# Attention and feed-forward in one kernel: values loaded two heads at a time, smaller steps, a second accumulator tile and a new list

## The chip, the cores and the metric

One core of a Trainium2 chip runs the whole program. A core has five engines, each with its own queue of instructions that it works off in order: TensorE (PE, matrix products, results in PSUM), VectorE (DVE), ScalarE (ACT), GpSimd (POOL) and SyncE (SP, which here issues every DMA). [...] The metric is the device time of the program in microseconds, median of the runs.

## The reference

Eight batches of windowed attention with eight heads of 64, 576 positions. Heads 0 to 3 see the 32 latest keys, heads 4 to 7 see every fourth of the latest 128. The attention's output goes through a two-layer feed-forward with float64 weights.

```python
scores = scale * np.matmul(q, k.transpose(0, 1, 3, 2))
mask_plain = (rel >= 0) & (rel < window)
mask_dil = (rel >= 0) & (rel < window * dilation) & (rel % dilation == 0)
scores = np.where(masks[None, :, :, :], scores, -1000000000.0)
attn = np.exp(scores - np.max(scores, axis=-1, keepdims=True))
attn = attn / (np.sum(attn, axis=-1, keepdims=True) + 1e-09)
x = np.matmul(attn, v)            # then laid out as [4608, 512]
h = x @ w_in                      # 512 -> 2048
g = h * np.tanh(softplus(h))
return (g @ w_out)                # 2048 -> 512
```

## The kernel before

The work is cut into 16 units, each half a batch: 288 positions, all eight heads. The plain heads are kind 0 (three blocks of 96 queries), the dilated ones kind 1 (four blocks, one for each residue). A unit runs through named steps. `ld` loads queries and keys, `lv` the values, `sp` makes the scores (PE), `sc` takes their maximum off (DVE), `ex` is the exponential (ACT), `tp` turns the probabilities, `va` multiplies them with the values (PE) and divides by their sum, `tx` turns the result into x, `ff` is the first layer (24 matmuls of 288 columns for each of eight steps). Up to unit 2 the second layer is `gt` and `fo` (four times 48 matmuls); from unit 3 on it is `ga`, `gq` and `fq`: seven products of half-size matrices in place of eight, of 144 columns each, on sums of weights (`su`) made once.

Units 0 to 2 are "direct": their probabilities and values are float32 and are turned on PE, since the weights are still being prepared. From unit 3 on both are split in two float16 parts and turned by a DMA transpose. Weights come as float64 and are made into two float16 parts in steps: `wl` loads, `wm` and `ws` find a scale, `ww` shifts words together (DVE L408, L410), `wp` splits (ACT L417, DVE L419). All this happens while the first units run.

What stands where in each engine's queue is set by hand: ORDER is a list of step names, and each name runs its generator to the next `yield`. A number behind `=` names the PSUM tile (of four, `b`) that the step takes. `kw` steps are matmuls of zeros that keep PE at work while it has nothing else.

The lines that the prediction speaks of: L494 and L497 load values; for each unit of half the positions that is 12 or 16 DMAs of 64 floats a row. In direct units L508 then copies them on POOL into rows of 65 with a one behind, so that one matmul also gives the sum. L573 are the scores, L598 and L599 the maximum and its subtraction, L606 and L608 the exponentials, L673 the values' matmuls, L681 to L689 the sum, its reciprocal and the quotient, L725 to L732 x of direct units, L715 to L720 x of the others. L773 is the first layer, L779 its Mish, L861 to L863 the gate of the first three units. L912 are the seven products, with three accumulators side by side in one PSUM tile; L926 (ACT) and L931 (DVE) read them into y. L961 is the second layer of units 0 to 2.

## Time and profile before

| what | us |
|---|---|
| median of 3 runs (lowest, highest) | 910.73 (908.52, 910.88) |
| the profiled execution | 902.42 |
| its span | 900.5 |
| PE busy in it | 848.4 (94%) |
| DVE busy | 638.4 (71%) |
| ACT busy | 472.4 (52%) |

The profiled execution is 8.3 us below the median of the timed runs, and 1.9 us above its own span. Durations below come from it. "Busy" of PE counts its matmuls, warming ones too; a wait is shown beside the instruction that waited, with the engine and line that ended it.

### The profile page before, as it was taken

What the parts mean: (1) busy time and instruction counts of PE and PEld (TensorE: products, weight loads), DVE (VectorE), ACT (ScalarE), POOL (GpSimd) and SP (SyncE); (2) the same over time, 40 slices, a digit from 0 to 9 for tenths busy, and PEclk for the clock granted to TensorE, in tenths of its full rate; (3) what the DMA queues carried; (4) which work ended last, traced back from release to release, by engine and by line L of the source; (5) the groups of instructions that cost most, each with busy time, mean ns of one, the idle gap of its engine ahead of it and who ended that gap; (6) DMA issues with size and microseconds to landing.
All of it is one profiled execution on the core that took longest, in us unless ns stands there. A gap on an engine that the chain in (4) does not pass through costs nothing. (4 is left out here: it accounts for less than half of the span.)

```text
span 900.5 us, 32620 instructions
## 1 busy us (share of the span) xinstructions
PE 848.4 (94%) x14897; PEld 724.8 (80%) x14897; DVE 638.4 (71%) x871; ACT 472.4 (52%) x641; POOL 101.6 (11%) x102
## 2 busy tenths in 40 slices
PE   6779998989999999999999899999999899999998
PEld 4656777867788888888887688888888788888987
DVE  5778977746899995878787858675778475744453
ACT  3364744652476565574745545545465275533342
POOL 6356452100000010000000100000000000000000
PEclk7889999999999999999999989999999899999999
DMA  9894252544321564356153443445252512210001
GB/s 278 245 257 117 92 177 59 105 120 119 71 52 19 124 143 87 92 121 136 41 127 82 116 71 66 108 90 108 59 110 73 93 41 51 52 36 23 15 15 41
DMA packets 194986, 86.33 MB, mean 96 GB/s; under 512 B 170272, under 2 KB 190752, under 8 KB 194848
## 3 DMA queue, kind: packets, MB, share of 16 engines
q1 hardware_dynamic: 194848, 84.25, 39.2%
q8 instruction: 116, 1.90, 0.9%
q14 instruction: 22, 0.18, 0.1%
HBM read 56.89 MB, written 9.44 MB: 74 GB/s over the span
## 5 line engine op out<-in xcount | busy, mean ns | idle before, releaser
L773 PE MATMUL b<-x,w 128*128 128x288 f16 x3072 | 400.2, 287 | 1.9 <-ACT den L683 0.5
L773 PEld LDWEIGHTS <-w 128*128 128x128 f16 x3072 | 294.4, 98 | 78.3 <-issue 3.2
L912 PE MATMUL b<-g,w 128*128 128x144 f16 x2496 | 166.6, 226 | 6.1 <-DVE y L931 4.5
L912 PEld LDWEIGHTS <-w 128*128 128x128 f16 x2496 | 158.4, 98 | 10.0 <-issue 6.3
L779 ACT ACTIVATE hm<-b,fs 128x576 f32<-128x576 f32 x128 | 92.4, 735 | 116.5 <-PE b L773 99.0
L886 DVE SCALAR_TENSOR_TENSOR g<-hm,sg,g 128x1152 f16<-128x1152 f32 (+1 forms) x104 | 130.9, 1270 | 31.5 <-PE b L773 16.5
L884 ACT ACTIVATE g<-hm,sg 128x1152 f16<-128x1152 f32 (+1 forms) x104 | 116.2, 1128 | 45.8 <-PE b L912 30.6
L931 DVE SCALAR_TENSOR_TENSOR y<-b,fo,y 128x144 f32<-128x144 f32 x78 | 33.5, 476 | 73.1 <-PE b L912 48.9
L926 ACT ACTIVATE y<-b,fo 128x288 f32<-128x288 f32 x52 | 40.5, 782 | 81.6 <-PE b L912 68.8
L476 POOL COPY qp<-qn 128x576 f32<-128x576 f32 x15 | 27.9, 1862 | 461.1 <-DMA qn<-in_qT 352.6
L892 DVE TENSOR_TENSOR hm<-hm 128x576 f32<-128x576 f32 x104 | 78.8, 769 | 0.9
L961 PE MATMUL b<-g,w 128*128 128x288 f16 x576 | 73.6, 286 | 2.7 <-ACT den L683 2.7
L961 PEld LDWEIGHTS <-w 128*128 128x128 f16 x576 | 55.6, 98 | 17.1 <-issue 2.9
L912 PE MATMUL b<-g,late_sums 128*128 128x144 f16 x936 | 68.4, 231 | 0.7 <-DVE y L931 0.7
L912 PE MATMUL b<-g,g 128*128 128x144 f16 x936 | 67.2, 227 | 1.3 <-issue 0.8
L912 PEld LDWEIGHTS <-late_sums 128*128 128x128 f16 x936 | 62.9, 100 | 1.9 <-DVE y L931 1.1
L912 PEld LDWEIGHTS <-g 128*128 128x128 f16 x936 | 61.0, 98 | 3.4 <-issue 1.7
L715 ACT CAST x<-xs 96x384 f16<-96x384 f32 (+1 forms) x52 | 29.1, 560 | 47.0 <-DMA x<-x 33.5
L687 DVE RECIPROCAL rec<-den 96x6 f32<-96x6 f32 (+1 forms) x64 | 12.0, 187 | 50.7 <-ACT den L683 46.2
L717 DVE TENSOR_TENSOR x<-xs,x 96x384 f16<-96x384 f32 (+1 forms) x52 | 32.1, 617 | 21.4 <-ACT x L715 21.4
L689 DVE TENSOR_TENSOR xs<-b,rec 96x384 f32<-96x384 f32 (+1 forms) x64 | 39.7, 621 | 6.9 <-PE b L725 1.1
L673 PEld LDWEIGHTS <-pT 64*32 64x32 f16 (+1 forms) x3276 | 30.0, 91 | 16.5 <-issue 8.1
(125 smaller groups left out, 838.9 us busy)
## 6 DMA issues: line engine op xcount, KB each, us to landing
qn<-in_qT SPq DMA_DIRECT2D x15, 576.0 KB, 4.5
vn<-in_vd SPq DMA_DIRECT2D x132, 64.0 KB, 2.8
raw<-in_w_out SPq DMA_DIRECT2D x16, 512.0 KB, 4.9
out_T<-y SPq DMA_DIRECT2D x26, 288.0 KB, 2.4
raw<-in_w_in SPq DMA_DIRECT2D x12, 512.0 KB, 4.9
vn<-in_v SPq DMA_DIRECT2D x28, 144.0 KB, 2.7
knd<-in_kdT SPq DMA_DIRECT2D x14, 224.0 KB, 3.2
vn<-in_v SPq DMA_DIRECT2D x24, 128.0 KB, 2.6
```

The lines of the kernel that those rows point to most:

```text
L673: nc.tensor.matmul(avv[s * SQ:(s + 1) * SQ, h, t], p[:hk.stop - hk.start], vv[vi][hk, window(d, kind, t, s), a, :], start=(i == 0), stop=( ...
L689: nc.vector.tensor_tensor(xs[:, :nb].rearrange("p j (h e) -> p h j e", h=2), avv[:, :, :, :D], rc.unsqueeze(3).broadcast_to([QB, 2, nb, D] ...
L717: nc.vector.tensor_tensor(lo, xs[:, :nb], hi, op=ALU.subtract)
L773: nc.tensor.matmul(ph[:, h, :HT], w1[j][:, c, wi, k * P:(k + 1) * P], x_of(d, xi, c), start=(n == 0), stop=(n == len(seq) - 1))
L779: nc.scalar.activation(d["m"][p][:, half, k0:k0 + 2], ph[:, :, :HT], AF.Mish, scale=d["fs"][:, j:j + 1])
L884: nc.scalar.activation(hi, src, AF.Identity, scale=sg)
L886: nc.vector.scalar_tensor_tensor(lo, src, sg, hi, ALU.mult, ALU.subtract)
L892: nc.vector.tensor_tensor(a, a, b, op=op)
L912: nc.tensor.matmul(acc[e], left(l, e, p, wi)[:, k * P:(k + 1) * P], right(gi, k), start=(n in opens and p == 0 and q == 0), stop=(last and ...
L926: nc.scalar.activation(into(half, t), by(acc), AF.Identity, scale=fo)
L931: nc.vector.scalar_tensor_tensor(o, by(acc)[:, e], fo, o, ALU.mult, ALU.add)
L961: nc.tensor.matmul(po[:, :HT], w2[:, e, j, wi, k * P:(k + 1) * P], d["g"][j][:, gi, k, :], start=(j == 0 and n == 0), stop=(j == NCH - 1 a ...
```

## The change

Values are loaded with one descriptor for two heads (128 floats in a row). A window's row now is one, 64 values, 64 values, one (VW = 130 wide), so both heads have their column of ones at an end, and direct units load straight into it: the copy on POOL is gone. Probabilities are laid out by head, then block. Scores stop after two blocks (a `yield`), values are made by blocks with both heads and both pairs together: three steps `va` in place of four (kind 0 whole, kind 1 in two pieces), each with a `yield` behind every block; x likewise. For units 0 and 1 the maximum is taken off by a matmul into PSUM with an identity, and the exponential reads PSUM. The warming matmuls multiply float32 ones, and there are 59 in place of 220. The seven products stand in another order, and one of the three accumulators has a PSUM tile of its own in every unit (before: in the last unit only). ORDER is new.

```diff
+    VW = 2 * (D + 1)
+    APART = range(16)
+    PE_MAX = (0, 1)
...
         if d["direct"]:
-            vn = w2[:, :2].rearrange("p e j i n -> p (e j i n)").bitcast(F32)[:, :NW * 2 * D]
+            vh = pool.tile([P, NW, VW], F32, tag="vh", name="vf", bufs=2)[:, :sum(nw)]
+            nc.gpsimd.memset(vh[:, :, ::VW - 1], 1.0)
+            vn = vh[:, :, 1:VW - 1]
...
-        for h in range(2):
-            for a in range(2):
-                c = (2 * a + h) * D
-                row = v[b, half * (HT - WIN), c:c + D]
-                o = vn[h * WK:(h + 1) * WK, :, a]
...
-        nc.gpsimd.tensor_copy(vh[:, :, :, :D], vn)
+        for a in range(2):
+            o = vn[a * WK:(a + 1) * WK]
+            row = v[b, half * (HT - WIN), 2 * a * D:2 * (a + 1) * D]
+            nc.sync.dma_start(o[:, :n0], bass.AP(row.tensor, row.offset, [[w, WK], [SQ * w, n0], [1, 2 * D]]))
+            yield
...
+        if u in PE_MAX:
+            yield
+            for h in range(2):
+                nc.tensor.matmul(pt[:QB, h, :n * w].rearrange("p (g k) -> p g k", k=w), ident[:QB, :QB],
+                                 nm[:, h, :n].unsqueeze(2).broadcast_to([QB, n, w]), start=False, stop=True,
+                                 skip_group_check=True)
+            d["src", kind], d["dst", kind] = src, dst
+        else:
+            nc.vector.tensor_tensor(dst, src, nm[:, :, :n].unsqueeze(3).broadcast_to([QB, 2, n, w]), op=ALU.add)
...
+    def span(p):
+        return (1, 2 * p - 2, 2 * p) if p else (0, 0, NPB)
...
-    PRODUCTS = (("11", 0, 0, 0), ("12", 0, 1, 2), (0, 3, 0, 1), (1, 2, 0, 0), (2, 3, 1, 0), (3, 1, 0, 1), ("22", 2, 1, 0))
+    PRODUCTS = (("12", 0, 1, 2), ("11", 0, 0, 0), (0, 3, 0, 1), (1, 2, 0, 0), (3, 1, 0, 1), (2, 3, 1, 0), ("22", 2, 1, 0))
...
-        apart = u == NU - 1
+        apart = u in APART
...
-            po[n:] = [take("b", banks)] * (3 - n) if n or not apart else [take("b", banks)] + po[1:]
+        if p == 0 and n == 0:
+            po[1:] = [take("b", banks)] * 2
+            if not apart:
+                po[0] = po[1]
+        if p == 0 and n == 1 and apart:
+            po[0] = take("b", banks)
...
-            nc.tensor.matmul(spare, zeros, zeros[:, :WIDE_MAX], start=not spared, stop=True, skip_group_check=True)
+            nc.tensor.matmul(spare, ones.broadcast_to([P, P]), ones.broadcast_to([P, WIDE_MAX]), start=not spared, stop=True, skip_group_check=True)
...
 ORDER = """
-wl0.0.1 wm0.0.1 mf ld0 ww0.0.1 qp0 ld0 mf cs1 kw43 sp0.0=0 cs0 wl0.0.0 ld0 ld0 ww0.0.0 ww0.0.1 wm0.0.0 ww0.0.1 ld1
+wl0.3.0 wl0.3.1 ld0 ld0 wm0.3.0 wl0.0.0 wm0.3.0 mf ww0.3.0 ww0.3.0 cs1 cs0 wm0.3.1 ld0 ld0 wl0.0.1 ww0.3.0 ww0.3.0
...
```

The first place is SP's queue at the program's start, which decides when the first values land. Before (`raw` are weights, `qn`/`qk` queries of units 0 and 1, `knp` and `knd` keys, `w_90` the place where values of direct units waited):

```order
L343 DMA raw<-in_w_in 128x512 x2
L461 DMA qn<-in_qT 128x1152
L466 DMA knp<-in_kT 128x2x288
L343 DMA raw<-in_w_in 128x512 x2
L470 DMA knd<-in_kdT 128x4x80 x2
L461 DMA qk<-in_qT 128x1152
L466 DMA knp<-in_kT 128x2x320
L343 DMA raw<-in_w_in 128x512 x2
L470 DMA qk<-in_kdT 128x4x112 x2
L494 DMA w_90<-in_v 64x8x64
L497 DMA w_90<-in_vd 64x4x64 x2
```

And SP's queue of the changed kernel, from its start (`vf` are the values in their final place):

```order
L347 DMA raw<-in_w_in 128x512 x4
L465 DMA qn<-in_qT 128x1152
L470 DMA knp<-in_kT 128x2x288
L347 DMA raw<-in_w_in 128x512 x2
L474 DMA knd<-in_kdT 128x4x80 x2
L347 DMA raw<-in_w_in 128x512 x2
L499 DMA vf<-in_v 64x8x128
L503 DMA vf<-in_vd 64x4x128 x2
L499 DMA vf<-in_v 64x8x128
L503 DMA vf<-in_vd 64x4x128 x2
L465 DMA qk<-in_qT 128x1152
L470 DMA knp<-in_kT 128x2x320
```

Two weight pieces (four DMAs) now stand ahead of the first queries, a fourth piece ahead of the values, and unit 1's queries and keys behind unit 0's values instead of ahead; the values are six DMAs in place of twelve.

The second place is DVE's queue where unit 0's attention ends: reciprocals and quotients of the values, and the lower halves of x, on which the first layer waits. Before:

```order
L687 RECIPROCAL rec<-den 96x2x3
L689 TENSOR_TENSOR xs<-b_73,rec 96x2x3x64
L687 RECIPROCAL rec<-den 96x8
L689 TENSOR_TENSOR xs<-b_72,rec 96x2x4x64
L687 RECIPROCAL rec<-den 96x2x3
L689 TENSOR_TENSOR xs<-b_71,rec 96x2x3x64
L408 SCALAR_TENSOR_TENSOR w_89<-w_89,raw 128x512
L687 RECIPROCAL rec<-den 96x8
L689 TENSOR_TENSOR xs<-b_70,rec 96x2x4x64
L410 SCALAR_TENSOR_TENSOR raw<-raw,w_89 128x1024
L732 TENSOR_TENSOR x<-b_72,x 128x4x3x24
L732 TENSOR_TENSOR x<-b_73,x 128x288
```

Now:

```order
L700 RECIPROCAL rec<-den 96x2x4
L702 TENSOR_TENSOR xs_636<-b_73,rec 96x512
L423 SCALAR_TENSOR_TENSOR w_89<-raw,ws_314,w_89 128x2x512
L414 SCALAR_TENSOR_TENSOR raw<-raw,w_86 128x1024
L598 TENSOR_REDUCE nm<-b_71 96x2x6
L412 SCALAR_TENSOR_TENSOR w_87<-w_87,w_90 128x1024
L700 RECIPROCAL rec<-den 96x2x4
L702 TENSOR_TENSOR xs_684<-b_72,rec 96x512
L412 SCALAR_TENSOR_TENSOR w_87<-w_87,w_90 128x1024
L743 TENSOR_TENSOR x<-b_70,x 128x2x192
L743 TENSOR_TENSOR x<-b_73,x 128x576
L743 TENSOR_TENSOR x<-b_72,x 128x2x192
```

More weight work (L412, L414, L423, which were L408, L410, L419) stands between the quotients, and a reduction of unit 1's scores is followed by no subtraction.

The third place is DVE's queue in unit 14, where the accumulators of the products are read into y. Before, all reads of a unit name one tile:

```order
L892 TENSOR_TENSOR hm<-hm 128x4x144
L886 SCALAR_TENSOR_TENSOR g_98<-hm,sg,g_98 128x1152
L931 SCALAR_TENSOR_TENSOR y<-b_73,fo,y 128x2x72 x2
L886 SCALAR_TENSOR_TENSOR g_100<-hm,sg,g_100 128x1152
L886 SCALAR_TENSOR_TENSOR g_99<-hm,sg,g_99 128x576
L931 SCALAR_TENSOR_TENSOR y<-b_73,fo,y 128x2x72 x2
L892 TENSOR_TENSOR hm<-hm 128x4x144
L886 SCALAR_TENSOR_TENSOR g_99<-hm,sg,g_99 128x576
L886 SCALAR_TENSOR_TENSOR g_97<-hm,sg,g_97 128x1152
L892 TENSOR_TENSOR hm<-hm 128x4x144 x2
L931 SCALAR_TENSOR_TENSOR y<-b_73,fo,y 128x2x72 x2
```

Now they name two:

```order
L949 SCALAR_TENSOR_TENSOR y<-b_71,fo,y 128x2x72 x2
L900 SCALAR_TENSOR_TENSOR g_100<-hm,sg,g_100 128x1152
L900 SCALAR_TENSOR_TENSOR g_99<-hm,sg,g_99 128x1152
L949 SCALAR_TENSOR_TENSOR y<-b_71,fo,y 128x2x72 x2
L900 SCALAR_TENSOR_TENSOR g_98<-hm,sg,g_98 128x576
L906 TENSOR_TENSOR hm<-hm 128x4x144
L900 SCALAR_TENSOR_TENSOR g_100<-hm,sg,g_100 128x1152
L906 TENSOR_TENSOR hm<-hm 128x4x144 x2
L900 SCALAR_TENSOR_TENSOR g_101<-hm,sg,g_101 128x1152
L900 SCALAR_TENSOR_TENSOR g_98<-hm,sg,g_98 128x576
L906 TENSOR_TENSOR hm<-hm 128x4x144
L949 SCALAR_TENSOR_TENSOR y<-b_73,fo,y 128x2x72 x2
```

Of four PSUM tiles a unit's products now hold two, and the reads of one no longer stand against matmuls into the other.

## Rows read from the trace of the kernel before

**Rows 1.** The page: busy time of each engine, its share of the span, instructions.

```profile
PE 848.4 (94%) x14897; PEld 724.8 (80%) x14897; DVE 638.4 (71%) x871; ACT 472.4 (52%) x641; POOL 101.6 (11%) x102
```

**Rows 2.** Busy time by stretch (start:end, length, PE, PEld, DVE, ACT, POOL, clock, DMA share, GB/s).

```profile
0.00:45.40 45.40, 31.19 (x767) 25.30 (x768) 29.82 (x45) 16.93 (x26) 21.61 (x39) 0.81 0.90 261
45.40:120.70 75.30, 67.44 (x991) 51.21 (x989) 64.32 (x97) 45.32 (x65) 38.09 (x19) 0.95 0.56 162
120.70:311.00 190.30, 181.91 (x2883) 147.97 (x2882) 152.41 (x204) 100.58 (x137) 24.46 (x20) 1.00 0.38 90
311.00:870.00 559.00, 541.73 (x9855) 474.56 (x9853) 376.85 (x508) 298.74 (x405) 17.42 (x26) 0.99 0.36 79
```

**Rows 3.** Timeline of PE: start, length, line, tiles, count, the idle time before.

```profile
29.98 1.40 PE L673 MATMUL b<-vf,pp 64*32 64x65 f32 x108 [1.49 <-POOL vf L508]
...
45.37 0.41 PE L773 MATMUL b<-x,w 128*128 128x288 f16 x2
...
120.74 6.04 PE L961 MATMUL b<-g,w 128*128 128x288 f16 x48
```

**Rows 4.** Timeline of POOL: the copy of unit 0's values.

```profile
28.03 1.89 POOL L508 COPY vf<-w 128x2048 f32<-128x2048 f32 x1 [9.79 <-DMA w<-in_vd]
```

**Rows 5.** Timeline of SP: first and last issue of unit 0's twelve value loads.

```profile
14.61 0.64 SPq L494 DMA_DIRECT2D w<-in_v  x1
...
24.38 1.68 SPq L497 DMA_DIRECT2D w<-in_vd  x2
```

**Rows 6.** Busy time around these loads.

```profile
12.00:20.00 8.00, 6.74 (x193) 4.54 (x192) 6.01 (x10) 2.15 (x5) 5.70 (x11) 0.65 1.00 281
20.00:28.00 8.00, 5.61 (x177) 4.80 (x175) 7.09 (x7) 3.99 (x5) 0.00 (x0) 1.00 0.77 124
```

**Rows 7.** Groups by line and shape: busy us, mean ns, idle before.

```profile
L419 DVE SCALAR_TENSOR_TENSOR w<-raw,ws,w 128x1024 f16<-128x1024 f32 x14 | 18.5, 1338 | 1.1 <-ACT w L417 1.0
...
L408 DVE SCALAR_TENSOR_TENSOR w<-w,raw 128x1024 int32<-128x1024 int32 x13 | 16.2, 1258 | 10.9 <-POOL raw L406 10.1 <-POOL w L363 0.7
...
L991 PE MATMUL b<-zeros 128*128 128x96 f16 x220 | 15.4, 243 | 6.4 <-DVE wm L384 3.1 <-ACT den L681 1.4 <-DVE zeros L984 1.0
...
L673 PE MATMUL b<-vf,pp 64*32 64x65 f32 x504 | 8.3, 230 | 5.3 <-POOL vf L508 3.5 <-issue 1.8
...
L599 DVE TENSOR_TENSOR sb<-b,nm 96x1024 f32<-96x1024 f32 x3 | 3.7, 1221 | 0.1
...
L599 DVE TENSOR_TENSOR sb<-b,nm 96x768 f32<-96x768 f32 x3 | 2.9, 954 | 0.2
...
L561 PE MATMUL b<-m_b,ident_b 96*96 96x512 bf16 x6 | 2.2, 455 | 2.3 <-POOL m_b L272 1.3 <-DVE x L732 1.0
```

**Rows 8.** Timeline of ACT: a table load and the instruction behind it.

```profile
98.72 1.28 ACT L779 ACT_TABLE_LOAD   x1
100.02 1.37 ACT L779 ACTIVATE hm<-b,fs 128x576 f32<-128x576 f32 x2
```

**Rows 9.** Who PE waited for: us in total, times, longest.

```profile
PE b L673 <- DMA pT<-p: 5.4, 2, 4.5
PE b L912 <- DVE y L931: 5.2, 8, 1.0
...
PE b L573 <- DMA knd<-in_kdT: 2.8, 1, 2.8
```

**Rows 10.** Busy time behind PE's wait at 711.

```profile
711.00:717.00 6.00, 5.54 (x148) 4.81 (x149) 4.29 (x5) 1.43 (x3) 0.47 (x2) 0.50 0.58 120
717.00:723.00 6.00, 6.00 (x160) 5.08 (x159) 0.98 (x4) 3.04 (x5) 0.00 (x0) 0.97 0.41 93
```

**Rows 11.** Timeline of SP ahead of that wait: value loads, then the keys' load.

```profile
702.96 0.62 SPq L494 DMA_DIRECT2D vn<-in_v  x1
703.64 2.41 SPq L497 DMA_DIRECT2D vn<-in_vd  x3
706.09 0.61 SPq L470 DMA_DIRECT2D knd<-in_kdT  x1
```

## The prediction

> **What bounds the kernel now.** First the page's busy times: PE is busy 94% of the span and no other engine over 71% [rows 1]. So time can only be won where PE waits, runs at the low clock or does filler. The view by stretch shows where that is [rows 2]. Up to the first matmul of the first layer at 45.4 [rows 3] PE is busy 31.2 us at a mean clock of 0.81, and 15.4 us in all are warming matmuls [rows 7]. From there to the first matmul of the second layer at 120.7 it idles 75.3 - 67.4 = 7.9 us, at 0.95, while DVE is busy 64.3 of 75.3 us, 85%. Between 120.7 and 311 it idles 8.4, and between 311 and 870, 17.3 us. The start is bound by the way of data and weights through POOL, ACT and DVE, the rest by PE, with waits strewn in. The list of waits names the ones that count [rows 9]: two on a turned probability tile (5.4 us, one of them 4.5), eight of a product's matmul on DVE reading y (5.2), one on keys (2.8).

> **The start.** The way to the first layer begins with unit 0's values. Before, their twelve loads are issued from 14.61 to 26.06 [rows 5], 0.95 us each, the transfers slow from 281 to 124 GB/s meanwhile [rows 6], the POOL copy starts at 28.03 [rows 4] and the first values' matmul at 29.98 [rows 3]. Now there is no copy and there are six loads. Against that stand two things. Ahead of the values SP has 2.1 MB of the last weight group, so the first scores come later: 3.0 MB up to unit 0's plain keys, of which the old order needed 1.9, and the 281 GB/s of rows 6 make the difference 4 us. And the loads now wait for POOL to write the ones, which stands behind a weight piece in POOL's queue; that I put at 17 us. Six issues at 0.95 end at 22.7, and landing took 2 us in rows 4 and 5 (26.06 to 28.03): 25 us for the last value. But unit 1's queries and keys (1.4 MB, 5 us at 281 GB/s) are loaded behind them, and on PE unit 1's dilated scores stand ahead of the last third of unit 0's plain values. That gives 30 for these scores, 31 for the third, 32.2 for DVE's reduction of the scores.

> From there I count DVE's queue, with the durations of the same forms before (1.34 and 1.26 us for a weight instruction, 0.95 and 1.22 for a score one, and so on) [rows 7]. Up to the last lower half of unit 0's x it has 14 instructions, 10.8 us: x is whole at 43, against 45.4 to 47.5, when the old one's first layer began and its x was done. Little is won there. More is won behind it: up to the second half of the first output weights, without which the second layer cannot go far, the new queue has 85 instructions, 65.8 us, so 55.0 behind x. DVE at the 85% of rows 2 takes 64.4 us for them: 107.5. PE has less to do in that time: 384 matmuls of the first layer at 0.126 us, the pace of the 48 in rows 3, are 48 us, and the scores, values and turns of units 1 and 2 are small beside that. So the second layer begins at 107.5 in place of 120.7. The old list had then also made unit 2's values and x (84 matmuls of two records each at 8.3 / 504 = 0.0165 us [rows 7], 2.8 us, and 14 float32 transposes, which I put at 1.5), which the new one has ahead of it: 120.7 - 4.3 - 107.5 = 8.9 us. I take 8; the bounds are 18, with a DVE that never idles, and 0, with one busy 75%. What shortens the queue is the subtraction of the maximum in units 0 and 1, 2 x (1.22 + 0.95) = 4.3 us of DVE [rows 7], and that weights which waited for values now stand ahead of them.

> What the start pays on PE: eight identity matmuls of 384 or 512 float32 columns. The trace has none. The nearest below is the bfloat16 one of 512 columns, where two took 0.6 us: 2.2 us for all eight; above, four times that, 8.8. They stand where PE waits for DVE anyway; with that cover gone they cost up to 8.8. The 59 warming matmuls of ones cost at least the 0.07 us of a float16 one [rows 7], 4 us together, at most four times as much, 17 us. 54 of them stand before the first scores, so they end at 5 to 17 us; the first scores' data come near 13. By the upper bound unit 0's scores start 4 us late, but its values land at 25, so I take nothing.

> Three more pairs of table loads for ACT come with exponentials that stand among Mish steps, one of them ahead of the second layer's start. The row shows 1.28 us for a load and the next ACTIVATE 0.02 us behind it [rows 8]; that is 2.6 us there and 7.7 us in the program, and ACT idles 30 of 75 us in that stretch [rows 2]: nothing. [...]

> **The products.** Before, the three accumulators share one PSUM tile, and where the last product follows its predecessor at once its matmuls wait until DVE has read y, up to 1.0 us [rows 9]. Now the accumulator that product adds to has its own tile, and counted in the new list at least 1.5 us of other matmuls stand between any product and the next one on its accumulator, with reads of 0.8 to 0.95 us. Of the 5.2 us I take 4; bounds 0 and 5.7.

> **What costs nothing.** The steady units have the same scores', values', first-layer and product matmuls, in count and size. DVE loses a quarter of the reciprocals and some calls (7 us of 638), POOL three copies, SP 77 issues of 0.6 us and more: none of them bounds PE between 311 and 870, where DVE is busy 67%. The half scores and block-wise values only let PE put other matmuls between.

> **What I cannot price.** The wait on keys at 711 came behind one plain and three dilated value loads, 3 us of SP [rows 11], and the landing of the keys. [...] I take 0, as the nearest thing, a different order over the same work, has no sign.

> **Sum.** -8 - 4 = -12 us. The profiled execution's own 902.4 us would be 890.4. The runs shown have a median 8.3 us above it, and I subtract the same from that: 910.7 - 12 = 898.7, say 899.

> **Rivals.**
> 1. The start wins nothing: the ones on POOL, unit 1's loads and the float32 filler hold unit 0 back, and DVE's idle share goes up where it waited less before. For it: the x of unit 0 comes only 2 to 4 us earlier by my own sum. Against it: DVE's shorter queue. Only the products are left: 910.7 - 4 = 907.
> 2. The long waits go too. For it: half as many value loads, each row 512 bytes, stand ahead of keys and turned tiles on SP [rows 11]. Against it: x now follows the last values' matmul within 10 to 14 us of matmul work in three units (shortest before 13), and some keys are loaded late. Time: 898.7 - 13 = 886.
> 3. The second accumulator tile makes the kernel slower. The products of a unit hold two of four tiles for some 42 us of matmuls (14 groups of 48, each at 0.063 us, half of the 288-column pace), so the first layer, scores and values of the next unit alternate on two. Counted in the lists by matmul time, a tile is taken again within 3.1 us of its last matmul 46 times of 166 now, 31 of 165 before; one ACT queue held up by a gate's 1.25 us or a table load then stops PE. For it: these counts. Against it: before, such waits are almost absent, though 31 places were that tight. Four stops like the one at 711 cost 4 x 5.8 = 23 us: 898.7 + 23 = 922. It decides from 0.9 us in each of 13 units on, which eats the 12 us.

> **How the numbers follow.** My forecast 0.47; rival 1 0.20; rival 2 0.17; rival 3 0.16. 0.3% (2.7 us, about what a measurement of this kernel can tell from no change) either side of 910.7 is 908.0 to 913.4. Faster: the forecast, rival 2 and half of rival 1, 0.74. Same: the other half of rival 1 and 0.02 of rival 3, 0.12. Slower: 0.14. The likeliest case's own range runs from 910.7 - 18 - 4 = 889 to 910.7 - 3, where the start wins 3 and the products nothing, 908. For 8 in 10 it has to reach to rival 2 and half into rival 3: 884 to 914.

> **What would show it.** Right: the first second-layer matmul between 103 and 113 us, unit 0's last value landed by 27, the wait list without matmuls of the products waiting for y, or with under 1.5 us of them, and 13 to 18 us of idle PE from the first steady unit's products to the last ones, where there were 17.3. Wrong: the second layer starting after 116 (rival 1); waits of first-layer matmuls on Mish, gates or y of over 10 us in sum, and more slices with a clock under 1.00 (rival 3); no wait over 2.5 us anywhere behind 311 (rival 2).

## The result, and the profile after

The changed kernel takes 868.06 us (median of 4 runs, 865.43 to 869.62), the kernel before beside it 910.81 (908.52 to 911.99): ratio 0.953, 95% interval 0.950 to 0.956. That is 43 us less where 12 were forecast, and 16 below the range. Measured again beside other runs of before (905.25, run e18 below) the unchanged new kernel gave 867.33 and 0.958 [0.954, 0.961]: before's own runs in all these comparisons spread from 897.5 to 913.5, so the gain is 38 to 43.

The page after: busy times; DMA packets; and the queue whose packets are code, of which more below.

```profile
PE 841.4 (97%) x14811; PEld 726.0 (84%) x14811; DVE 635.5 (74%) x818; ACT 479.2 (56%) x615; POOL 91.0 (11%) x99
DMA packets 154886, 86.29 MB, mean 100 GB/s; under 512 B 92288, under 2 KB 150656, under 8 KB 154752
q8 instruction: 116, 1.90, 1.0%
```

Against [rows 1], PE is busy 7.0 us less, and the span is 37.0 shorter. The views by stretch say where. After, cut at the first matmul of the first layer, of the second layer, of the products, and at the last product (columns as in [rows 2]):

```profile
0.00:52.10 52.10, 41.86 (x698) 31.93 (x699) 29.05 (x43) 20.12 (x29) 18.42 (x39) 0.87 0.98 269
52.10:112.70 60.60, 58.93 (x796) 46.24 (x795) 59.37 (x76) 41.14 (x51) 31.12 (x15) 1.00 0.65 168
112.70:249.30 136.60, 134.65 (x2189) 108.31 (x2187) 108.17 (x146) 70.78 (x94) 24.06 (x16) 1.00 0.48 102
249.30:859.30 610.00, 605.74 (x11136) 539.50 (x11134) 438.88 (x557) 346.42 (x442) 17.42 (x29) 1.00 0.39 78
```

Before, from the second layer to the first product and to the last; the two stretches ahead are in [rows 2]:

```profile
120.70:261.00 140.30, 133.91 (x2023) 106.54 (x2022) 104.77 (x144) 70.31 (x99) 22.64 (x19) 1.00 0.41 98
261.00:895.90 634.90, 615.62 (x11124) 541.77 (x11122) 438.60 (x587) 339.84 (x455) 19.24 (x27) 0.99 0.35 76
```

The first product comes 11.7 us earlier, and from it to the last 24.9 are won: 15.0 of PE's idle time (19.3 to 4.3) and 9.9 of its busy time over the same work. About half of the 9.9 is the clock. Before, PE ran twice at 0.50 behind a long wait, at 711 [rows 10] and here:

```profile
516.00:522.00 6.00, 3.90 (x82) 3.83 (x83) 1.08 (x2) 0.83 (x2) 0.12 (x1) 0.50 1.34 187
```

At 0.50, 24 matmuls of 144 columns took 3.0 us (from 712.49), at 1.00 48 of them did (from 524.81). At twice the clock these two stretches would have been some 5 us shorter (an estimate: half of PE's 5.54 and 3.90 us of busy time in them); after, the clock of the whole stretch is 1.00. Where the rest of the 9.9 lies is not traced. So two thirds lie where the forecast had only the products' 4 us. PE's waits in that stretch after, all of them that the view lists; of [rows 9], DVE's y and the keys are gone:

```profile
PE b L686 <- DMA pT<-p: 1.6, 2, 0.9
PE b L787 <- issue: 1.0, 1, 1.0
PE b L575 <- issue: 0.9, 1, 0.9
PE b L930 <- ACT g L898: 0.5, 1, 0.5
PE b L930 <- ACT y L944: 0.2, 1, 0.2
```

### The profile page after: what moved, and what is told of

The parts are those of the page before. It is cut to its first block, busy times and chain, and to the rows that moved or that the text cites. A ratio compares the mean times of both kernels' runs of the same rounds, so it can differ in the third digit from the quotient of the medians.

```text
span 863.5 us, 32177 instructions
## 1 busy us (share of the span) xinstructions
PE 841.4 (97%) x14811; PEld 726.0 (84%) x14811; DVE 635.5 (74%) x818; ACT 479.2 (56%) x615; POOL 91.0 (11%) x99
## 2 busy tenths in 40 slices
DMA packets 154886, 86.29 MB, mean 100 GB/s; under 512 B 92288, under 2 KB 150656, under 8 KB 154752
## 4 chain that ended last, share of the span: by engine, by line
PE 79%; DVE 8%; DMA 5%; issue 3%; SPq 2%; ACT 2%; POOL 1%; DVEq 0%; POOLq 0%; ACTq 0%
PE b L787 37%; PE b L930 27%; PE b L969 6%; PE b L686 3%; DMA pT<-p 3%; PE b L575 3%; DVE w L423 1%; SPq L503 1%; DMA qk<-in_kdT 1%; DMA raw<-in_w_in 1%; DVE vh L543 1%; DVE w L412 1%; DMA vn<-in_vd 1%; DVE nm L598 1%; PE b L602 1%
## 5 line engine op out<-in xcount | busy, mean ns | idle before, releaser
L787 PE MATMUL b<-x,w 128*128 128x288 f16 x3072 | 392.2, 286 | 2.7 <-issue 1.0
L480 POOL COPY qp<-qn 128x576 f32<-128x576 f32 x15 | 29.1, 1942 | 438.5 <-DMA qn<-in_qT 407.0
L930 PE MATMUL b<-g,late_sums 128*128 128x144 f16 x936 | 65.9, 226 | 0.0
L930 PEld LDWEIGHTS <-late_sums 128*128 128x128 f16 x936 | 60.0, 98 | 0.6
L726 DVE TENSOR_TENSOR x<-xs,x 96x512 f16<-96x512 f32 (+1 forms) x39 | 30.2, 773 | 20.2 <-ACT x L724 20.2
L702 DVE TENSOR_TENSOR xs<-b,rec 96x512 f32<-96x512 f32 (+1 forms) x48 | 37.2, 776 | 5.1 <-PE b L735 0.7
L543 DVE SCALAR_TENSOR_TENSOR vh<-vn,s,vh 128x2688 f16<-128x2688 f32 (+1 forms) x13 | 36.0, 2768 | 3.4 <-ACT vh L541 3.2
L724 ACT CAST x<-xs 96x512 f16<-96x512 f32 (+1 forms) x39 | 26.8, 686 | 20.1 <-DMA x<-x 12.6
```

What stands on the lines that cost most here:

```text
L543: nc.vector.scalar_tensor_tensor(lo, src, s, hi, ALU.mult, ALU.subtract)
L702: nc.vector.tensor_tensor(xs.rearrange("p (a t h e) -> p a t h e", a=2, h=2, e=D), avv[:, :, :, 1:VW - 1].rearrange("p a t (h e) -> p a t ...
L787: nc.tensor.matmul(ph[:, h, :HT], w1[j][:, c, wi, k * P:(k + 1) * P], x_of(d, xi, c), start=(n == 0), stop=(n == len(seq) - 1))
L930: nc.tensor.matmul(acc[e], left(l, e, p, wi)[:, k * P:(k + 1) * P], right(gi, k), start=(n in opens and p == 0 and q == 0), stop=(last and ...
```

## Experiments

"Products" is the time from the first product's matmul to the last, in the profiled run (two profiles of the unchanged new kernel gave 610.0 and 613.2); "code" is what PE waits in it for nothing that another engine ends ("issue").

| run | us | ratio to before | first product | products | code |
|---|---|---|---|---|---|
| before | 904 to 911 | 1 | 261.0 | 634.9 | 2.9 |
| after (first comparison) | 868.1 | 0.953 [0.950, 0.956] | 249.3 | 610.0 | 1.9 |
| e1 64-float value rows | 879.9 | 0.972 [0.965, 0.980] | 247.9 | 624.5 | 1.0 |
| e2 one tile in 7 units | 882.7 | 0.974 [0.968, 0.980] | 248.1 | 627.7 | 2.6 |
| e3 whole values, scores | 870.2 | 0.961 [0.954, 0.967] | 250.3 | 615.3 | 5.4 |
| e4 maximum on DVE | 865.9 | 0.956 [0.950, 0.962] | 248.0 | 611.6 | 3.0 |
| e5 before, wide rows | 896.7 | 0.988 [0.982, 0.994] | 261.6 | 629.0 | 7.5 |
| e6 wide rows, twice the loads | 879.4 | 0.969 [0.963, 0.976] | 249.0 | 623.8 | 1.7 |
| e7 e1, e2 and e3 | 895.8 | 0.988 [0.982, 0.994] | 248.0 | 641.0 | 3.0 |
| e8 5 warming matmuls for 54 | 888.8 | 0.980 [0.974, 0.987] | 254.2 | 628.2 | 17.5 |
| e9 e8 and 49 short ones | 873.7 | 0.968 [0.962, 0.973] | 253.9 | 613.1 | 2.8 |
| e10 15 short ones more | 893.3 | 0.989 [0.982, 0.995] | 257.8 | 627.8 | 15.4 |
| e11 32 short ones more | 925.4 | 1.026 [1.019, 1.033] | 267.5 | 642.1 | 28.4 |
| e12 before, 64 short ones more | 901.7 | 0.998 [0.995, 1.001] | 268.0 | 627.1 | 2.2 |
| e13 half a code block more | 911.3 | 1.007 [1.004, 1.009] | 265.7 | 644.6 | 29.1 |
| e14 a whole code block more | 867.5 | 0.959 [0.954, 0.965] | 249.4 | 612.9 | 3.0 |
| e15 e8, 98 short bfloat16 | 866.8 | 0.959 [0.954, 0.963] | 248.8 | 612.0 | 3.0 |
| e16 e4, 16 short bfloat16 | 865.3 | 0.957 [0.952, 0.962] | 245.3 | 611.1 | 2.2 |
| e17 e15 and e16 | 863.8 | 0.954 [0.950, 0.958] | 246.5 | 614.2 | 4.7 |
| e18 after, again | 867.3 | 0.958 [0.954, 0.961] | 250.7 | 613.2 | 2.9 |

### The value loads: e1, e6, e5

e1, from unit 3 on:

```diff
+        parts = ((0, 2 * D),) if d["direct"] else ((0, D), (D, D))
...
-            row = v[b, half * (HT - WIN), 2 * a * D:2 * (a + 1) * D]
...
+            for c, m in parts:
+                row = v[b, half * (HT - WIN), 2 * a * D + c:2 * a * D + c + m]
```

> The kernel after (868.1 us, 0.953 of before; 25 us of the gain lie between the first product and the last one), but from unit 3 on each value load is issued as two of 64 floats a row, one for each head, as before: twice the loads and descriptors, everything else in its place. Theory A, the place in the list: the long waits went because the list puts the work elsewhere; undoing the rows costs under 4 us, 868 to 872, and the waits on pT and keys stay under 1.5 us each. Theory B, the loads: half as many value loads ahead of keys and turned tiles in SP's queue is what took the long waits away; 878 to 893, with waits on pT or knd of over 2.5 us back and PE at clock 0.50 behind them.

e6, the other way to twice the loads (m is half of the windows; the dilated values likewise):

```diff
+            for j in range(0, n0, m):
+                k = min(m, n0 - j)
+                nc.sync.dma_start(o[:, j:j + k], bass.AP(row.tensor, row.offset + j * SQ * w, [[w, WK], [SQ * w, k], [1, 2 * D]]))
```

> The kernel after, from unit 3 on with each value load cut in two along its windows: rows of 128 floats as in the kernel after, the same number of rows, but twice as many loads on SP, as in e1. Theory A, the count of loads on SP (0.6 us and more each ahead of keys and turns) is what e1 paid for: as e1, 876 to 884. Theory B, the length of the rows, so the number of descriptors and their time in the DMA engines: 866 to 870, as the kernel after.

Both cost the same, 11.8 and 11.3 us, though only e1 has short rows (187,464 packets, 156,360 in e6, 154,886 after). So it is the count of loads, not the length of the rows. SP around one unit's loads, after:

```profile
331.43 0.62 SPq L499 DMA_DIRECT2D vn<-in_v  x1
332.11 1.95 SPq L503 DMA_DIRECT2D vn<-in_vd  x3
...
336.75 2.69 SPq L503 DMA_DIRECT2D vn<-in_vd  x3
```

and in e6:

```profile
333.48 1.30 SPq L502 DMA_DIRECT2D vn<-in_v  x2
334.82 4.83 SPq L508 DMA_DIRECT2D vn<-in_vd  x6
...
343.96 3.86 SPq L508 DMA_DIRECT2D vn<-in_vd  x6
```

From the start of the first issue to the end of the last it is 8.0 us there and 14.3 here, loads of keys between them included. The transfers themselves are no slower: a turned tile lands 4.3 us after its issue in e6 and 4.1 in the new kernel (medians). So what needs the loads, and what stands behind them on SP, is issued late, and PE waits (e6, whole program; line 329 spreads the values' maximum over the partitions, 691 are the values):

```profile
PE b L691 <- DMA pT<-p: 3.7, 3, 2.5
...
PE b L329 <- DVE m L525: 3.0, 1, 3.0
```

e5 lays heads 0, 2, 1, 3 side by side in DRAM, so that the old kernel's loads become half as many with 128 floats a row:

> The kernel before, old list and all, with one edit: heads lie in DRAM so that a value load takes rows of 128 floats, half as many loads, as in the kernel after (POOL's copy for direct units stays). Theory A, loads by themselves: what undoing them cost in the kernel after (11 us, 14.5 between first and last product) is won here; ratio to before 0.983 to 0.992, waits on knd and pT of 2.8 and 5.4 us gone. Theory B, list and loads fit each other: the old list was set for its own loads, the gain is under 4 us, ratio 0.995 to 1.005.

Theory A: 9.4 us by the medians, on the old list too. The wait on keys is gone, and that on pT falls from 5.4 [rows 9] to 2.3 us. Its profile has 5.9 us fewer in the products, though code waits there rose from 2.9 to 7.5. The start does not move (45.4, 121.1 and 261.6). No run issued the loads on another queue than SP's.

### The second tile, the pieces, the maximum: e2, e3, e7, e4

e2 (`SHARED` maps units 3, 7, 9, 10, 11, 12 and 14 to the tile that stays free longest; the other six could not be tried, since the list gives the tile to others meanwhile):

```diff
+        if opens and u in SHARED:
+            po[:] = [banks[SHARED[u]]] * 3
```

> The kernel after, but in seven of the thirteen units with products (3, 7, 9, 10, 11, 12, 14) the three accumulators lie in one PSUM tile again; the order of the products stays. Theory A: the order of the products (at least 1.5 us between two on one accumulator) took the 5.2 us of waits on y, the tile of its own does nothing by itself: 866 to 870. Theory B: reading one accumulator holds up products into its neighbours in the same tile; 7 units by 0.4 to 1.0 us each, 3 to 7 us more, 871 to 875, with waits of the product line on y.

14.6 us, twice what theory B allowed, 2 us a unit. The waits in e2:

```profile
PE b L929 <- ACT y L943: 6.2, 6, 1.9
PE b L929 <- DVE y L948: 4.7, 5, 1.1
```

10.9 us on reads of an accumulator beside the one written, with the order of the products as in the new kernel. With the tile apart these waits are 0.2 us in the new kernel; the old list, with one tile and its own order of products, paid 5.2 us of DVE's [rows 9]. So the new list leans on the tile more than the old one would have; that it sets products closer because of it is the likely reason and was not tried by itself. Whether it is the chip or the program's own semaphores that hold PE there was not told apart.

e3 issues all blocks of a value step where the first stood, and scores likewise:

```diff
-            yield
+            if d["direct"]:
+                yield
+        for t in range(t0, t1):
+            if not d["direct"]:
+                yield
```

> The kernel after, but from unit 3 on the scores of a kind and the blocks of a value step are all issued where their first piece stood, and nothing where the others stood: the same matmuls, no other work between. Theory A, smaller pieces are what fills PE: work that PE could do while ACT or DVE free a tile is gone from between; 7 to 15 us more, 875 to 883, with idle PE from 4.2 us to over 10 between 311 and the last product. Theory B, only the places of whole steps count: 866 to 871 and under 6 us idle there. Theory C, as rival 3 of the prediction: pieces hold PSUM tiles longer, so issuing at once is faster, 860 to 866.

2.1 us by the medians, no more than two profiles of one kernel differ. Theory A is out; little more can be said. Of the 5.3 us more in its profile's products, 3.5 are code waits (5.4 for 1.9), not waits for a tile.

> The kernel after with e1, e2 and e3 together: 64-float value rows, one PSUM tile in seven units, no smaller pieces, so that of the change the list, the order of the products and the start are left. If the costs add up between first and last product (14.5 + 17.7 + 5.3 = 37.5 us over 610.0): 903 to 908, no faster than before, and the list has no gain of its own. If they share the same waits: 885 to 895, and the list keeps some 15 to 25 of the 43 us.

27.7 us, just above the second range. The medians of e1 to e3 add up to 28.5, so the three hardly share waits; my 37.5 came from single profiles and was too high (in this profile it is 31.0). Against the runs of before beside it (906.1) e7 is still 10.4 us faster, and that lies at the start: the first product comes at 248.0, 13.0 earlier than before, while the products take 641.0 us, 6.1 longer than before. So the new list without the wide loads and the tile is worse there than the old one, and what undoing costs in it is more than what the two brought.

e4: `PE_MAX = ()`.

> The kernel after, but the maximum of units 0 and 1 is taken off by DVE, as before, not by eight identity matmuls on PE (8.7 us of PE). Theory A, DVE's queue sets the start: 4 subtractions of 0.95 to 1.22 us more, the first second-layer matmul 4 us later (112.7 to 117) and the end 2 to 5 us later, 870 to 873. Theory B, PE's own filler and clock set it: PE is 8.7 us freer, 861 to 868. Theory C: cover, 867 to 869.

No loss: the four subtractions go back into DVE's queue, and the second layer still starts at 111.7 (109.9 in e16 below; 112.7 and 114.8 in the two profiles of the new kernel). Taking them out of that queue did not make the start faster.

### Where PE's code is cut: e8 to e14

e8 puts `kw5` for `kw54` in the list.

> The kernel after with 5 in place of 54 warming matmuls ahead of unit 0's scores (54 ran from 0.9 to 15.0 us in the kernel after). Theory A: scores start earlier by what the warming holds them back, at most 2 us, end 866 to 868. Theory B: they end before the data are there, and without them the clock of the scores and of the first turns stays at 0.50 for longer; 868 to 872, mean clock of the stretch before the first layer under the 0.89 of the kernel after.

Neither: 20.8 us slower, 18.2 of them in the products, 200 us after the edit. PE's waits in that stretch of e8:

```profile
PE b L930 <- issue: 10.3, 9, 1.9
PE b L787 <- issue: 4.4, 3, 2.3
PE b L686 <- issue: 2.8, 1, 2.8
```

e9, e10 and e11 put float32 matmuls of one column behind the warming ones (`kw5 kt49`, `kw54 kt15`, `kw54 kt32`):

```diff
+    def short(n):
+        for _ in range(n):
+            nc.tensor.matmul(spare[:, :1], ones.broadcast_to([P, P]), ones, start=not spared, stop=True, skip_group_check=True)
...
```

> e8 lost 20.8 us, of them 18 between first and last product, where nothing was changed: 17.8 us of waits that nothing on another engine ends, each about 128 matmuls (256 PE instructions) or a multiple of it behind the last, each 1.3 to 1.6 us behind the landing of a 16 KB instruction packet. Theory P, code blocks: PE's code comes in blocks of 256 instructions; a block that PE runs through in under some 3.5 us, as one full of 16 ns value matmuls, ends before the next block is there; without 49 warming matmuls the blocks are cut elsewhere in the program. Theory W, warming: the start runs at a lower clock and what follows lands differently. This kernel is e8 with 49 matmuls of one column put where the warming ones were: as many instructions as in the kernel after, hardly any work. P: 866 to 871, and issue waits between first and last product of 2 to 3 us as in the kernel after. W: 884 to 892, as e8.

> The kernel after with 15 float32 matmuls of one column (two passes, 30 records, some 2 to 4 us) more behind the 54 warming ones, where PE waits for data anyway. All cuts between code blocks move 30 matmuls ahead in the program. From the trace of the kernel after, blocks cut so that run under 3.6 us would lack 22 us in sum, 3.6 as it is. Theory P (code blocks): 880 to 890, with 10 to 20 us of issue waits between first and last product. Theory W: 867 to 871.

> The same with 32 such matmuls, 64 records, half a block. Blocks under 3.6 us would lack 47 us in sum. Theory P: 890 to 912, so that 32 matmuls of one column give back half of the gain of the change or all of it. Theory W: 868 to 873.

Theory P in the products each time: 613.1, 627.8, 642.1 us. But the totals are 3 to 13 us above it. The fillers were not short, which may be why: 64 records took 10.2 us in e11, 98 took 21.0 in e9. So e13 and e14 took bfloat16 (`ones_b`), `kw54 kt64` and `kw54 kt128`:

> The kernel after with 64 bfloat16 matmuls of one column (some 0.03 us each, 2 us together) behind the warming ones: 128 PE instructions, half a code block. In e11, between first and last product, the same shift cost 32.1 us (642.1 against 610.0), and its fillers another 18 ahead of the first product. Theory P, code blocks: 35 to 45 us slower than the kernel after, 903 to 913, 25 to 30 us of issue waits between first and last product. Theory F, it was the fillers' 10 us at the start that upset everything behind: 869 to 874.

> The same with 128 of them, some 4 us: 256 PE instructions, one whole block, so that every cut lies where it lay, one block later. Theory P: back to the kernel after, 868 to 873, under 4 us of issue waits between first and last product. Theory F: worse than e13.

Half a block costs 43 us, a whole one nothing. No order is changed, no wait added, 128 matmuls of one column are faster than 64. The 43 are not in the products alone: ahead of the first one PE's code waits are 20.0 us in e13, most of them ahead of values (the line below), against 5.5 in the new kernel, and the first product comes 16.4 later.

```profile
PE b L686 <- issue: 15.7, 3, 6.8
```

In e13's products, four stretches from one such wait to the next:

```profile
339.05:363.33 24.28, 19.82 (x384) 17.03 (x385) 13.32 (x17) 9.73 (x11) 3.42 (x3) 1.00 0.71 136
363.33:445.17 81.84, 80.02 (x1535) 68.63 (x1534) 61.92 (x78) 48.47 (x62) 6.09 (x6) 0.98 0.55 100
445.17:477.74 32.57, 30.83 (x512) 27.31 (x513) 24.48 (x34) 23.05 (x29) 0.00 (x0) 1.00 0.29 53
477.74:488.28 10.54, 8.54 (x256) 8.23 (x257) 8.48 (x11) 5.57 (x8) 0.00 (x0) 1.00 0.88 135
```

PE's counts are 3, 12, 4 and 2 times 128, one short once. And the wait at 363.33:

```profile
357.31 1.56 PE L686 MATMUL b<-vh,pT 56*32 56x65 f16 x166
363.33 0.35 PE L686 MATMUL b<-vh,pT 64*32 64x65 f16 x14 [4.46 <-issue]
```

The whole block before the cut is values, of 166 in 1.56 us, so it was over in 1.3; its successor's packet started at 360.58, took 1.16 and PE went on 1.59 later. In the new kernel the same values stand astride a cut, with first-layer matmuls on both sides. Not every short block stops PE. Between e13's first and last such wait in the products the eleven blocks that took under 2 us all did, and of the ten from 2.0 to 2.7 us four did.

e12 does it to the kernel before (`kw43 kt64`, float16 zeros):

> The control: the kernel before with 64 float16 matmuls of one column behind its first 43 warming ones, half a block too. In its list the small matmuls don't stand at a fixed distance in blocks: by its trace 7 to 10 us are lacking wherever the cuts are (9.0 as it is, 7.3 half a block on). Theory P, with the new list alone set to its cuts: ratio to before 0.995 to 1.006. If the old list were set to its cuts as well: 1.015 or more.

No difference in the whole: the first product comes 7.0 us later, the products take 7.8 less. The old list lies no better to its cuts than to those half a block on. The new list does.

### The start: e15 to e18

e15 is `kw5 kt98`, e16 `PE_MAX = ()` with `kw54 kt16`, e17 both with `kw5 kt114`, all bfloat16.

> The kernel after with 5 of the 54 warming matmuls, and 98 bfloat16 matmuls of one column for the other 49 (98 records): cuts as in the kernel after, about 11 us less filler on PE before unit 0's scores. If warming does nothing: scores up to 2 us earlier and no issue waits more, 864 to 869. If the clock or the flow of the start needs it: first matmul of the first layer later than 53 and 870 to 876.

> e4 (maximum on DVE in units 0 and 1) with 16 bfloat16 matmuls of one column in place of the 16 records of the identity matmuls that it lost, so that the cuts lie as in the kernel after. e4 as it was took 865.9, with 3.0 us of issue waits between first and last product. If its cuts cost it something: 862 to 866. If not: 866 to 869.

> e15 and e16 together: 5 warming matmuls in place of 54, the maximum on DVE in units 0 and 1, and 114 bfloat16 matmuls of one column so that the cuts lie as in the kernel after. If both gains at the start are real and add: 862 to 865, first product at 244 to 246 (249.3 in the kernel after, 248.8 in e15, 245.3 in e16). If the start is bound by data either way: 865 to 868, as e18.

> The kernel after unchanged, beside the same runs of before as e17: 866 to 869, ratio 0.955 to 0.960 if the 910.8 of its first comparison was a high day for the kernel before.

With the cuts kept, the warming can go. e15 differs from e8 by 98 short matmuls alone, so e8's loss came from its cuts. e17 is the fastest median, 3.5 us under e18 beside it, but the intervals of the two ratios overlap. The first product came 4.2 earlier than in e18's profile.

## Why the prediction was wrong

**The start: its sign came true, partly by luck.** The second layer begins at 112.7 (103 to 113 was "right"), SP issues unit 0's values from 17.70 (17 was said), and PE's last wait on them ends at 25.78 (by 27). But "x is whole at 43" failed: it is at 53.3, and the first layer begins at 52.1, 6.7 later than before. PE stands 4.3 us at a code cut, goes on at 0.50 until 48, and DVE waits for it:

```profile
25.78 0.44 PE L686 MATMUL b<-vf,pp 64*32 64x65 f32 x22 [0.89 <-DMA vf<-in_v]
36.84 2.18 PE L686 MATMUL b<-vf,pp 64*32 64x65 f32 x106 [4.34 <-issue]
36.84:48.00 11.16, 9.94 (x193) 6.42 (x193) 5.93 (x8) 4.17 (x7) 2.21 (x2) 0.50 1.06 238
46.46 0.95 DVE L598 TENSOR_REDUCE nm<-b 96x12 f32<-96x768 f32 x1 [3.42 <-PE b L575]
52.04 1.22 DVE L743 TENSOR_TENSOR x<-b,x 128x576 f16<-128x576 f32 x2 [0.37 <-ACT x L741]
```

Behind x the queue took 59.4 us, not 64.4: DVE was busy 98% of it (59.37 of 60.60 us from the first layer on), where 85% was assumed. The two errors, 10 late and 5 gained, left the second layer 5 behind the 107.5, just inside the sign. The step "8.9, I take 8" counted to the second layer; there it was 120.7 - 112.7 - 4.3 = 3.7. By the first product it is 11.7, as PE's idle time between these two falls from 6.4 to 1.95. That stretch I had not counted. "What shortens the queue is the subtraction" is not borne out (e4, e16), and half as many loads don't move the start of the old list (e5). The new list with its order of the weights' steps, the dropped copy and the smaller steps of the direct units are left as causes; no run tried any of them by itself.

**What the start pays: right.** The 54 warming matmuls came near the upper bound (they end at 15.0 us, 17 was the most), the identity matmuls took it (8.7 of 8.8), and without them the medians are no more than 3 us lower (e15, e16):

```profile
0.92 14.12 PE L996 MATMUL b<-ones 128*128 128x96 f32 x108 [0.92 <-DVE ln_p L988]
...
L602 PE MATMUL b<-nm,ident 96*96 96x384 f32 (+1 forms) x16 | 8.7, 673 | 0.9 <-DVE nm L598 0.9
```

**"SP 77 issues ...: none of them bounds PE": the step that failed.** It took only the engines' busy time. But keys and turned probabilities stand in the same queue behind the value loads, and a load takes the issuing queue 0.6 us [rows 11]. Twice the loads cost the new kernel 11 us (e1, e6), half of them gave the old list 9 (e5). (The count was off too: from unit 3 on the pages have 184 value loads before and 92 after.)

**"What I cannot price ... I take 0": the other half of the same step.** The long waits went, and rival 2 had the reason. It got 0.17, and its sign came true: behind 311 no wait is over 2.5 us, the longest is 1.0. Its 13 us were about right: waits on turned tiles fell by 3.8 us, those on keys by 2.8, and the clock behind them gave some 5. No run shows the 13, or rival 3's 5.8 for a stop, as such: shown are waits of 4.5 and 2.8 us [rows 9] and a clock of 0.50 in 6 us around each ([rows 10], and the line at 516 above). The idle time forecast as "right", 13 to 18 us, is 4.3. Its 886 still lacked the start's other 4 us and what else went in the products.

**The products: -4, bounds to 5.7.** Its own waits went as said, 5.2 us of DVE's y and 0.3 of ACT's. But the tile was priced by the waits that the old list had left, not by what a new list needs it for: taken away in seven units it costs 14.6 us. That is its price in the new list, not its gain over the old one. Rival 3, that it makes things slower, is refuted.

**Pieces:** nothing, as said, within 2 us (e3).

In sum, by the two profiles, whose spans differ by 37.0: the start gave 11.7, the products 24.9. Of these, 5.5 are waits on y, 3.8 on turned tiles, 2.8 on keys, 3 other waits, some 5 the clock, and nearly 5 of PE's busy time are open. The costs of undoing (loads 11, tile 15, pieces 2) don't divide the gain, as e7 shows.

No part of the prediction had the code cuts. They don't make the gain: those waits are 4.5 us ahead of the first product and 2.9 in the products before, 5.5 and 1.9 after. But they are its condition. Half a block on, the new kernel is slower than the old one.

## What to carry to other kernels

A queue that issues DMAs is a resource of its own (here 0.6 us an issue, and 11 us for twice the value loads): count its issues ahead of the transfer that PE waits for, and halve those first. A tile that frees the order can be worth more to a new order than the waits that the old one left (here 14.6 us in seven units, against 5.2). On a PE that is hardly ever idle (97% busy here), look for "issue" waits a multiple of 128 matmuls apart (here up to 6.8 us each), keep the number of PE instructions ahead the same when variants are compared, and shift it on purpose, by half a block (here 43 us) and a whole one (nothing), before a slower variant is blamed on its edit.

## What the runs showed of the hardware

- PE can stop where it runs through a block of 256 instructions in a short time (1.3 to 4.3 us ahead of the waits looked at in the products; in e13 every block under 2 us): up to 6.8 us a time, 20 us ahead of the products of e13 and 29 in them.
- A float32 matmul of one column cost no less than one of 96: 64 records in 10.2 us (e11) and 98 in 21.0 (e9), where 108 records of 96 columns took 14.1 (after) and 64 float16 or bfloat16 ones of one column 1.8 (e12, e13).
- Twice as many value loads for the same bytes, in rows of the same length, cost 11 us (e6); each takes SP's queue 0.6 us.
- Before's own median went from 904 to 911 us between comparisons: effects under 1% need before and after side by side.
